# A routing search that starts tighter: next expert's first span from the running expert's first round, three rounds instead of four for experts 3 to 5

## The chip, the cores and the metric

One NeuronCore of one Trainium2 chip. The metric is the device time of one execution in microseconds (us); the kernel before takes 852.79 us, the median of three runs (852.39 to 853.32). Engine names: PE is TensorE (PEld its weight loads), DVE is VectorE, ACT is ScalarE, POOL is GpSimd, SP is SyncE.

## The reference

Windowed attention with sink tokens gives `x` (3072 tokens of 512). A first mixture of experts (top one of eight by `x @ w_gate + bias`) replaces `x`. A second mixture, the one that matters here, gives every one of its eight experts exactly `cap` = 384 tokens, greedily by score:

```python
logits = x @ w_gate
order = np.argsort(-logits.flatten())
for idx in order:
    tok, e = idx // E, idx % E
    if assigned[tok] >= 0 or counts[e] >= cap: continue
    assigned[tok] = e; counts[e] += 1
for e in range(E):
    mask = assigned == e
    out[mask] = np.maximum(x[mask] @ w1[e], 0) @ w2[e]
```

## The kernel before

**Order of the work.** Attention, then the first mixture, then the second (`moe2`, from about 497 us on). In `moe2` the eight experts' feed-forward blocks run one after the other in the order in which the experts fill up; expert k below means the k-th to fill. Each block has eight steps (`Ffn.run`); a step is 12 matmuls of the first layer (L1036) and 9 of the second (L950), all in three-way split fp32. During the last two steps of a block the rows of the next expert are transposed on PE (L796) after three indirect gathers on POOL have fetched them (L1893).

**The routing.** It is not done ahead: `Route.steps` is a generator that is advanced between groups of matmuls of the blocks, so that expert k+1 and k+2 are searched while expert k computes. For each expert it searches the score at which the best-filled expert reaches 384 tokens. One round of the search divides the present span into 62 parts: DVE forms `ub` and compares it with 64 marks (`compare`, L1678 and L1679, the tile `cmp`), PE counts with 13 matmuls (`count`, L1693), DVE compares the counts with 384 (`gs`, `gg`), PE sums over partitions with one matmul (L1976), DVE takes the maxima (`J8`, one value per expert in falling order) and forms the new lower end `lo`. Between rounds POOL copies one number (`hold`, L1957): it depends on DVE's `b0`, so POOL, which works in order, does not begin what is queued behind it (the weight splits L901 and L922) until DVE has done its comparison. Then the expert's rows are marked (`A`), turned into a list of indices by `compact_steps` (L1498, L1517, L1523, `idx`), and POOL gathers them.

**Number of rounds.** `NIT` is 4. Expert 0 takes three rounds (1 to 3, the first was done earlier by `Route.pre`), experts 1 and 2 take three (0 to 2), experts 3 to 6 take four (0 to 3), expert 7 gets what is left. The lower end of expert k's first span is `lb[k]`, from the one coarse round of `Route.pre`; its upper end is the threshold of expert k-1.

**What sets the order.** Every instruction is queued by hand-written order. A planner (`Clock`, `Vec`) counts the matmul columns as PE time and adds for each routing instruction on DVE 0.12 us and 1.04 ns for each element of its free size. After each piece of the routing the generator yields the planned time at which its next piece may be queued (`yield clk.dve + CM[...]`, `CM` 0.2, 1.3, 1.3). `Route.pop`, called several times in each step, queues the next piece if that time has come and DVE is not planned ahead of PE by more than `SLACK`. Gathers for expert j are queued when its list is ready and the blocks have come to step 8j-9 (`poll_x`, `XO`).

The instructions of `steps`, `compact_steps` and others that are recorded through `Vec` all carry L145 in the profile (the helper's line), so that they are told apart by their tiles.

Of the kernel before, what the change touches and what calls it, by code (L numbers as in the profile page):

```python
# [15 lines left out]
OP = mybir.AluOpType  # L16
# [9 lines left out]
E, F = 8, 1024  # L26
# [32 lines left out]
def bc(ap, shape):  # L59
    return ap.to_broadcast(shape)  # L60


class K:
    def __init__(self):
        self.clk = Clock()
# [1401 lines left out]
JC, NIT, FEW, IDLE = 64, 4, 2, (3, 2, 1)  # L1467
WARM, WARM1, WA = 9, 3, (7, 4, 3, 2)
SLACK = 0.5
SLACK1 = 1.6  # L1470
XO = 9
X0 = 2.0
# [78 lines left out]
class Route(Src):  # L1551
# [4 lines left out]
    def __init__(self, nc, g, pool, xs):  # L1556
        self.nc, self.g, self.p, self.xs = nc, g, pool, xs
        self.e, self.regs, self.idx, self.x = {}, {}, {}, {}
        self.gen = self.steps()
        self.comp = []  # L1560
        self.em3 = {}
        self.at = [0.0, 0.0]
        p = pool
        self.L = p.tile([128, NR, E], F32, name="L")
        self.LG = p.tile([128, NSUB, E], F32, name="LG")
        self.ent = p.tile([128, NSUB, 2], I32, name="ent")
        self.pn = p.tile([128, NMAIN], F32, name="pn")
        self.vb = p.tile([128, NMAIN], BF, name="vb")
        self.tki = p.tile([128, 3, NMAIN], I32, name="tki")
        self.S_ = p.tile([128, NR], F32, name="S_")  # L1570
        self.OH = p.tile([128, NR, E], BF, name="OH")
        self.ub = p.tile([128, NR], BF, name="ub")
        self.cmp = p.tile([128, 2, JC, HR], BF, name="cmp")
        self.cuts = ((0, HA), (HA, HT + 1))
        self.cmp2 = [p.tile([128, 2, JC, e - o], BF, name=f"cmp{o}") for o, e in self.cuts]
        self.T = p.tile([128, NR], F32, name="T_")
        self.sc = p.tile([128, 20], F32, name="sc")
        self.fl = p.tile([128, E], F32, name="fl")
        self.lb = p.tile([128, E], F32, name="lb")
        self.pad = p.tile([128, SSML], F32, name="pad")  # L1580
        self.pw = p.tile([128, NIT], F32, name="pw")
        self.dd1 = p.tile([128, 4, NIT], F32, name="dd1")
        self.hold = p.tile([1, NIT], F32, name="hold")
        self.of = p.tile([2, 128], F32, name="of")
        self.z = p.tile([128, 128], BF, name="z")
        self.r = p.tile([128, 4, NR], F32, name="r0")
        self.gg = p.tile([128, E], BF, name="gg")
        self.gg2 = p.tile([128, 2, E], BF, name="gg2")
        self.tm = p.tile([128, NR], F32, name="tm")
        self.chk = p.tile([128, 3, E], F32, name="chk")  # L1590
        self.want = p.tile([128, 3, E], F32, name="chw")
        (self.lo0, self.lo, self.lop, self.b0, self.b1, self.J, self.esum, self.eidx, self.bad, self.t0, self.nbig, self.span,
         self.half, self.nrow, self.hi, self.J2, self.nv) = (self.sc[:, i:i + 1] for i in range(17))

    def setup(self):

# [56 lines left out]
    def sizes(self, V, pd):  # L1653
        V.tensor_reduce(self.half, pd, axis=AX.X, op=OP.max)
        V.tensor_scalar(self.nbig, self.half, 1e-20, -16.0, op0=OP.max, op1=OP.mult)
        V.tensor_scalar(self.half, self.nbig, 0.5, None, op0=OP.mult)
        V.tensor_scalar(self.nrow, self.nbig, 2.0, None, op0=OP.mult)

    def widths(self, V, dd, o, span):
        V.tensor_scalar(dd[:, 0, o:NIT], self.pw[:, 0:NIT - o], span, 1e-30, op0=OP.mult, op1=OP.max)  # L1660
        V.reciprocal(dd[:, 1, o:NIT], dd[:, 0, o:NIT])
# [167 lines left out]
    def pop(self):  # L1829
        clk = self.g.clk  # L1830
        for i, f in ((1, self.pop_comp), (0, self.pop_main)):
            if clk.pe >= self.at[i] and clk.dve < clk.pe + (SLACK if 1 in self.idx else SLACK1):
                f()
# [80 lines left out]
    def steps(self):  # L1914
        nc, g, p = self.nc, self.g, self.p
        clk = g.clk
        V = Vec(nc, clk)
        ioE = g.iota[:, 0:E]
        L, S_, OH, cmp, chk, tm = self.L, self.S_, self.OH, self.cmp, self.chk, self.tm
        lo, lop, b0, b1, esum, eidx, bad, t0, nbig, span, half, nrow = (  # L1920
            self.lo, self.lop, self.b0, self.b1, self.esum, self.eidx, self.bad, self.t0, self.nbig, self.span,
            self.half, self.nrow)
# [5 lines left out]
        J8 = p.tile([128, E], F32, name="J8m")  # L1928
        J = J8[:, 0:1]
        dn = None  # L1930
        for k in range(E):
# [4 lines left out]
            if k < E - 1:  # L1936
                dd = self.dd1 if k == 0 else dn
                lo0 = self.lb[:, k:k + 1]
                first = 1 if k == 0 else 0
                last = NIT - 1 if k == 0 or k > FEW else NIT - 2  # L1940
                for it in range(first, last + 1):
                    d, inv = dd[:, 0, it:it + 1], dd[:, 1, it:it + 1]
                    if k == 0:
                        if it > first:
                            V.scalar_tensor_tensor(self.ub, bc(dd[:, 2, it - 1:it], [128, NR]), J, self.T, op0=OP.mult, op1=OP.add)
                            self.against(V)
                            V.scalar_tensor_tensor(lo, J, dd[:, 0, it - 1:it], b0, op0=OP.mult, op1=OP.add)
                        if it < last:
                            V.tensor_scalar(b1, dd[:, 3, it:it + 1], lo, None, op0=OP.add)
                            V.tensor_scalar(self.T, S_, b1, dd[:, 1, it + 1:it + 2], op0=OP.subtract, op1=OP.mult)  # L1950
                        if it == first:
                            V.tensor_scalar(b0, d, -1.5, lo, op0=OP.mult, op1=OP.add)
                    else:
                        self.compare(V, slice(0, 2), slice(0, HR), inv)
                        V.tensor_scalar(b0, d, -1.5, lo0 if it == 0 else lo, op0=OP.mult, op1=OP.add)
                        if it > 0:
                            nc.gpsimd.tensor_copy(self.hold[:, it - 1:it], b0[0:1])  # L1957
                        if it < last:
                            V.tensor_scalar(b1, dd[:, 0, it + 1:it + 2], -128.0, b0, op0=OP.mult, op1=OP.add)
                    if k == 0 and it == first + 1:  # L1960
                        z = self.z
                    self.fill((0 if k == 0 else WT[7] if k == 1 else WT[0]) if it == first else WT[9 if it == first + 2 else 0] if k == 0 else WT[8])
                    yield clk.dve + CM[min(k, 2)]
                    self.count(pn, range(HT + 1), k == 0 and it > first)
                    clk.mm(64 * (HT + 1))
                    if it == first:
                        nc.tensor.matmul(pc, g.ones, OH, start=True, stop=True, skip_group_check=True)
                        nc.scalar.activation(junk, pc, AF.Copy, accum_out=chk[:, 0, k:k + 1])
                    gg = self.gg
                    V.tensor_scalar(gs, pn[JC:2 * JC, E:2 * E], -1.0, float(CAP) - 0.5, op0=OP.mult, op1=OP.add)  # L1970
                    V.tensor_tensor(gg[0:JC], pn[0:JC, 0:E], gs, op=OP.is_ge)
                    if k == 0 and it > first:
                        V.tensor_scalar(b0, d, -1.5, lo, op0=OP.mult, op1=OP.add)
                    self.fill(WT[1])
                    yield clk.dve + 0.2
                    nc.tensor.matmul(pb, g.ones, gg, start=True, stop=True, skip_group_check=True)  # L1976
                    V.max(J8, pb)
                    if k == 0 and it == first + 1:
                        nc.tensor.matmul(self.cbank[:, 0:64], z, z[:, 0:64], start=True, stop=True, skip_group_check=True)
                    if k > 0:  # L1980
                        if it < last:
                            V.scalar_tensor_tensor(lop, J, d, b1, op0=OP.mult, op1=OP.add)
                        V.scalar_tensor_tensor(lo, J, d, b0, op0=OP.mult, op1=OP.add)
# [297 lines left out]
```

## Time and profile before

| | us |
|---|---|
| median of three runs | 852.79 |
| profiled execution, its time | 853.57 |
| profiled execution, its span | 851.8 |
| PE busy | 813.5 (96%) |
| DVE busy | 608.7 (71%) |
| POOL busy | 348.0 (41%) |

The span is what the trace covers; 1.8 us of the profiled execution lie outside it. A window of the trace gives the busy time of each engine in a stretch, a timeline gives the instructions of an engine in order, with the idle time just before an instruction and what ended it in brackets.

### The profile page before, as it was taken

Reading aid. Unit: us, or ns where it says so; the run is one execution under the profiler, and the core shown is the slowest. Engines: PE = TensorE matmul, PEld = TensorE weight load, DVE = VectorE, ACT = ScalarE, POOL = GpSimd, SP = SyncE. Lnnn points to the kernel's source line nnn. Section 1 sums busy time; section 2 is a strip of 40 time slices with the busy share of each in tenths; the row PEclk is TensorE's granted clock in tenths of the full one; section 3 lists DMA queues with packets and bytes.
Section 4 is the critical chain, followed back from the end, with each engine's and each line's share of the span. In section 5 each row is a group of like instructions: output and inputs, shape, how many; then the busy total and the mean of one; then the engine's idle time right before and its main releaser. Section 6 shows DMA issues by size and latency. Waiting matters only on the chain.

```text
span 851.8 us, 15197 instructions
## 1 busy us (share of the span) xinstructions
PE 813.5 (96%) x5001; PEld 651.6 (76%) x5006; DVE 608.7 (71%) x1763; ACT 384.9 (45%) x1091; POOL 348.0 (41%) x574
## 2 busy tenths in 40 slices
PE   8889999998999999999999988999999999999997
PEld 4666666667888888888888746778888888889996
DVE  7888787877579696978878268868688787753320
ACT  6667777764342433344342313334334343434442
POOL 5455967582331101020000004436465656465662
PEclk9999999999999999999999998999999999999999
DMA  7434555666534544444436507334444345345401
GB/s 222 159 107 150 151 144 143 176 217 215 120 84 166 161 136 149 149 148 126 124 104 223 192 14 235 126 110 149 145 155 146 129 151 154 126 161 174 147 39 42
DMA packets 70655, 122.85 MB, mean 144 GB/s; under 512 B 9890, under 2 KB 24102, under 8 KB 70440
## 3 DMA queue, kind: packets, MB, share of 16 engines
q1 hardware_dynamic: 63848, 102.36, 38.0%
q0 software_dynamic: 6720, 19.43, 7.1%
q8 instruction: 42, 0.69, 0.4%
q14 instruction: 45, 0.37, 0.2%
HBM read 102.06 MB, written 19.71 MB: 143 GB/s over the span
## 4 chain that ended last, share of the span: by engine, by line
PE 78%; DVE 11%; ACT 4%; issue 3%; DMA 1%; POOL 1%; DVEq 0%; POOLq 0%; ACTq 0%
PE y L950 29%; PE ph L1036 28%; PE sp L323 4%; PE po L395 3%; ACT P L352 3%; PE tr L796 2%; PE rt L1693 2%; PE pt L360 2%; PE px L431 1%; PE rc L1523 1%; DMA xg<-xs,idx 1%; DVE mx L342 1%; DVE sc L145 1%; PE sp L409 1%; DVE sp L340 1%
## 5 line engine op out<-in xcount | busy, mean ns | idle before, releaser
L1046 ACT ACTIVATE hh<-ph 128x384 fp32r<-128x384 f32 (+1 forms) x112 | 60.2, 538 | 268.2 <-PE ph L1036 267.6
L1036 PE MATMUL ph<-xh,w1h 128*128 128x384 f32 (+1 forms) x448 | 166.9, 372 | 0.8 <-DVE hl L1047 0.8
L1036 PE MATMUL ph<-xh,w1l 128*128 128x384 f32 (+1 forms) x448 | 161.1, 360 | 1.2 <-DVE w1l L922 1.2
L1036 PE MATMUL ph<-xl,w1h 128*128 128x384 f32 (+1 forms) x448 | 160.4, 360 | 0.0
L950 PE MATMUL y<-w2h,hh 128*128 128x512 f32 x384 | 153.6, 400 | 0.0
L950 PE MATMUL y<-w2h,hl 128*128 128x512 f32 x384 | 150.9, 393 | 0.0
L950 PE MATMUL y<-w2l,hh 128*128 128x512 f32 x384 | 150.5, 392 | 0.0
L1047 DVE SCALAR_TENSOR_TENSOR hl<-ph,hh 128x384 fp32r<-128x384 f32 (+1 forms) x112 | 68.4, 612 | 98.6 <-ACT hh L1046 98.1
L1201 POOL DMA_INDIRECT xg<-xd,ent x26 | 28.0, 1078 | 195.0 <-DMA ent<-idtab 189.8
L1225 DVE SCALAR_TENSOR_TENSOR junk<-yr,wgb 128x512 f32<-128x512 f32 x160 | 103.1, 685 | 0.0
L901 POOL TENSOR_TENSOR w2l<-w2r,w2h 128x512 fp32r<-128x512 f32 x60 | 79.2, 1326 | 46.1 <-ACT w2h L897 22.2
L1036 PEld LDWEIGHTS ph<-xh,w1h 128*128 128x128 f32 x448 | 85.0, 190 | 12.6 <-issue 1.9
L1036 PEld LDWEIGHTS ph<-xh,w1l 128*128 128x128 f32 x448 | 84.3, 188 | 11.1 <-DVE w1l L922 1.6
L352 ACT ACTIVATE P<-sp,mx 128x132 f32<-128x132 f32 x192 | 69.3, 369 | 51.5 <-DVE mx L342 18.7
L1036 PEld LDWEIGHTS ph<-xl,w1h 128*128 128x128 f32 x448 | 84.0, 188 | 7.7
L950 PEld LDWEIGHTS y<-w2h,hl 128*128 128x128 f32 x384 | 72.0, 188 | 15.6
L950 PEld LDWEIGHTS y<-w2h,hh 128*128 128x128 f32 x384 | 72.6, 189 | 11.5 <-issue 0.2
L950 PEld LDWEIGHTS y<-w2l,hh 128*128 128x128 f32 x384 | 72.2, 188 | 11.7
L323 PE MATMUL sp<-kr,qs 64*128 64x260 f32 (+1 forms) x384 | 58.6, 402 | 13.7 <-ACT P L352 12.5
L917 ACT ACTIVATE w1h<-w1r 128x512 fp32r<-128x512 f32 x108 | 67.3, 624 | 2.1 <-DVE lp L449 2.1
L897 ACT ACTIVATE w2h<-w2r 128x512 fp32r<-128x512 f32 x108 | 67.5, 625 | 0.0
L922 DVE TENSOR_TENSOR w1l<-w1r,w1h 128x512 fp32r<-128x512 f32 x78 | 63.8, 818 | 2.4 <-ACT w1h L917 2.4
(394 smaller groups left out, 1401.9 us busy)
## 6 DMA issues: line engine op xcount, KB each, us to landing
w1r<-in_w_dram SPq DMA_DIRECT2D x29, 1024.0 KB, 5.8
w2r<-in_w_dram SPq DMA_DIRECT2D x29, 1024.0 KB, 5.9
vr<-in_v_dram SPq DMA_DIRECT2D x16, 384.0 KB, 4.9
xd<-xb SPq DMA_DIRECT2D x16, 384.0 KB, 3.5
xs<-yr SPq DMA_DIRECT2D x24, 256.0 KB, 6.1
kr<-in_kT_dram SPq DMA_DIRECT2D x15, 396.0 KB, 3.8
qr<-in_qT_dram SPq DMA_DIRECT2D x15, 384.0 KB, 4.3
wgb<-in_wg2T_dram SPq DMA_DIRECT2D x1, 2048.0 KB, 8.4
```

The costliest lines, as they stand in the source:

```text
L323: nc.tensor.matmul(sp[:, hd, c0:260], qs[o:o + 64, 128 * i:128 * i + 128], kr[o:o + 64, k0:k0 + 260 - c0], start=True, stop=True)
L352: nc.scalar.activation(z.P[:, n % 2, hd, :], s.sp[:, hd, 128:260], AF.Exp, bias=s.mx[:, hd:hd + 1], accum_out=z.sm[:, n % 2, hd:hd + 1])
L897: nc.scalar.activation(ch[1][c][0], r[q // 2][:, q % 2, :] if isinstance(r, list) else r[:, q, :], AF.Copy)
L901: eng.tensor_tensor(lo, r[q // 2][:, q % 2, :] if isinstance(r, list) else r[:, q, :], h.bitcast(F32), op=OP.subtract)
L917: nc.scalar.activation(h, v, AF.Copy)
L922: eng.tensor_tensor(lo, v, h.bitcast(F32), op=OP.subtract)
L950: nc.tensor.matmul(o, l, r, start=(first and i == 0), stop=(end and i == 2))
L1036: nc.tensor.matmul(ph, wp[:, c, :], xp_[:, c, 0:NTK], start=(d == 0 and i == 0), stop=(d == 3 and i == len(cut[d]) - 1))
L1046: nc.scalar.activation(hh, ph, AF.Relu)
L1047: nc.vector.scalar_tensor_tensor(hl, ph, 0.0, hh.bitcast(F32), op0=OP.max, op1=OP.subtract)
L1201: self.nc.gpsimd.indirect_dma_start(out=self.xg[j][:, a, :], out_offset=None, in_=self.G.xd[0:k, :], in_offset=bass.IndirectOffsetOnAxis(a ...
L1225: nc.vector.scalar_tensor_tensor(junk, yr[:, 0:DM], 1.0, wgb[:, e, :], op0=OP.mult, op1=OP.mult, accum_out=lg[:, e:e + 1])
```

## The change

One more instruction in `sizes` (once, before the routing begins) sets `least`, 0.04 of the largest score. In round 1 of experts 1 to 4 four more DVE instructions, each on a column of 128 numbers, raise the lower end `lb` of the next expert: the second-best expert's lower end after round 0, or the running expert's present lower end less `least`, whichever is lower, and never below the old one (if no second expert has reached 384 anywhere, the old one stays). Experts 3, 4 and 5 take three rounds instead of four. Expert 6 keeps four, experts 0, 1 and 2 keep three.

```diff
+LEAST = 0.04
@@ __init__
-         self.half, self.nrow, self.hi, self.J2, self.nv) = (self.sc[:, i:i + 1] for i in range(17))
+         self.half, self.nrow, self.hi, self.J2, self.nv, self.next, self.least, self.none) = (self.sc[:, i:i + 1] for i in range(20))
@@ sizes
+        V.tensor_scalar(self.least, self.nbig, -LEAST / 16.0, None, op0=OP.mult)
@@ steps
-                last = NIT - 1 if k == 0 or k > FEW else NIT - 2
+                last = NIT - 1 if k in (0, E - 2) else NIT - 2
...
                         self.compare(V, slice(0, 2), slice(0, HR), inv)
+                        if it == first + 1 and k < E - 3:
+                            low = self.lb[:, k + 1:k + 2]
+                            V.tensor_scalar(self.none, J8[:, 1:2], 0.5, nbig, op0=OP.is_lt, op1=OP.mult)
+                            V.tensor_scalar(self.next, J8[:, 1:2], dd[:, 0, first:it], b0, op0=OP.mult, op1=OP.add)
+                            V.scalar_tensor_tensor(self.next, lo, self.least, self.next, op0=OP.subtract, op1=OP.min)
+                            V.scalar_tensor_tensor(low, self.next, self.none, low, op0=OP.add, op1=OP.max)
                         V.tensor_scalar(b0, d, -1.5, lo0 if it == 0 else lo, op0=OP.mult, op1=OP.add)
```

## Rows read from the trace of the kernel before

**Rows 1.** The page's first part: engine, busy us (share of span), instructions.

```profile
PE 813.5 (96%) x5001; PEld 651.6 (76%) x5006; DVE 608.7 (71%) x1763; ACT 384.9 (45%) x1091; POOL 348.0 (41%) x574
```

**Rows 2.** Windows of 20 us: length, busy us of each engine, PE clock, DMA.

```profile
core 0: us, PE busy (x) PEld busy (x) DVE busy (x) ACT busy (x) POOL busy (x), PEclk, DMA share, GB/s
600.00:620.00 20.00, 20.00 (x115) 17.59 (x116) 15.66 (x47) 9.92 (x22) 8.83 (x11) 1.00 0.45 157
...
660.00:680.00 20.00, 18.93 (x143) 16.36 (x142) 15.61 (x38) 5.80 (x15) 13.37 (x14) 1.00 0.40 137
...
780.00:800.00 20.00, 20.00 (x103) 18.14 (x102) 5.29 (x8) 9.03 (x18) 12.42 (x12) 1.00 0.50 186
```

**Rows 3.** Timeline of PE, one round of expert 4: start, us, instruction.

```profile
629.36 0.95 PE L1693 MATMUL rt<-OH,cmp 128*128 128x16 bf16 x13
630.16 0.42 PE L1036 MATMUL ph<-xh,w1h 128*128 128x384 f32 x1
630.42 0.34 PE L1036 MATMUL ph<-xh,w1l 128*128 128x384 f32 x1
630.60 0.33 PE L1036 MATMUL ph<-xl,w1h 128*128 128x384 f32 x1
...
631.29 0.18 PE L1976 MATMUL rt<-gg,ones 128*128 128x8 bf16 x1
631.34 0.43 PE L1036 MATMUL ph<-xh,w1h 128*128 128x384 f32 x1
631.60 0.34 PE L1036 MATMUL ph<-xh,w1l 128*128 128x384 f32 x1
```

**Rows 4.** Timeline of PE, the fourth rounds' counts of experts 3, 4 and 5.

```profile
607.90 0.95 PE L1693 MATMUL rt<-OH,cmp 128*128 128x16 bf16 x13
...
643.93 0.96 PE L1693 MATMUL rt<-OH,cmp 128*128 128x16 bf16 x13
...
682.42 0.95 PE L1693 MATMUL rt<-OH,cmp 128*128 128x16 bf16 x13
```

**Rows 5.** Timeline of PE and its weight loads: instructions that waited, idle in brackets.

```profile
529.74 0.45 PE L1036 MATMUL ph<-xh,w1h 128*128 128x384 f32 x1 [0.79 <-DVE hl L1047]
...
555.25 0.33 PE L796 MATMUL tr<-cst,xg 128*128 128x128 f32 x1 [1.13 <-DMA xg<-xs,idx]
...
563.34 0.31 PEld L796 LDWEIGHTS tr<-cst,xg 128*128 128x128 f32 x3 [0.55 <-DVE xl L798]
...
599.96 0.33 PE L796 MATMUL tr<-cst,xg 128*128 128x128 f32 x1 [1.02 <-DMA xg<-xs,idx]
...
676.68 0.95 PE L1693 MATMUL rt<-OH,cmp 128*128 128x16 bf16 x13 [1.07 <-DVE cmp L145]
...
735.90 0.26 PE L2033 MATMUL rc<-OH,ones 128*128 128x224 bf16 x1 [0.68 <-DVE OH L145]
```

**Rows 6.** Timeline of DVE: routing instructions on one column.

```profile
576.66 0.21 DVE L145 TENSOR_TENSOR sc<-sc,lb 128x1 f32<-128x1 f32 x1
576.90 0.23 DVE L145 TENSOR_SCALAR dd<-pw,sc 128x4 f32<-128x4 f32 x1
...
593.40 0.35 DVE L145 SCALAR_TENSOR_TENSOR sc<-J8m,dd,sc 128x1 f32<-128x1 f32 x2
...
672.11 3.18 DVE L145 SCALAR_TENSOR_TENSOR sc<-J8m,dd,sc 128x1 f32<-128x1 f32 x2
```

**Rows 7.** Timeline of DVE behind round 1 or 2's comparison, experts 1, 2, 3.

```profile
529.14 1.01 DVE L1047 SCALAR_TENSOR_TENSOR hl<-ph,hh 128x384 fp32r<-128x384 f32 x2
...
562.74 0.55 DVE L798 TENSOR_TENSOR xl<-tr,xh 128x384 fp32r<-128x384 f32 x1
...
590.75 0.76 DVE L145 SCALAR_TENSOR_TENSOR idx<-pj 128x3 int32<-128x3 f32 x2
```

**Rows 8.** Timeline of POOL: a hold, a gather for expert 2, a weight split.

```profile
589.99 0.18 POOL L1957 COPY hold<-sc 1x1 f32<-1x1 f32 x1 [1.54 <-DVE sc L145]
...
592.82 1.02 POOL L1893 DMA_INDIRECT xg<-xs,idx  x1 [0.16 <-issue]
...
673.86 1.28 POOL L901 TENSOR_TENSOR w2l<-w2r,w2h 128x512 fp32r<-128x512 f32 x1
```

## The prediction

> **What bounds the kernel now.** I read the page's first part, then windows of 20 us over the second mixture, then the timelines of PE, DVE and POOL there. PE is busy 96% of the span [rows 1]. [...] So what the change takes out of PE's queue counts nearly one for one, unless PE then waits instead. The few waits are read one by one, since each is a place where a later DVE or POOL instruction moves the end. Between the start of the routing and its end those that matter are [rows 5]: 0.79 us for `hl` in expert 0's first steps; 1.13 for the last of expert 1's gathered rows (and a little less for those before them); 0.55 at a weight load, about half of it idle on PE, for `xl` at 563.34; 1.02 for expert 2's gathered rows; 1.07 for a `cmp` of expert 5; 0.68 for expert 7's `OH`. After the last list there is none: the window from 780 to 800 us is full and has no routing in it [rows 2].
>
> **What is removed.** Three rounds: the fourth ones of experts 3, 4 and 5, with their counts at 607.90, 643.93 and 682.42 [rows 4]. What a round costs PE is read from [rows 3]. The 13 counts push the block from 629.36 to 630.16, 0.80 us; the block's next two matmuls then start 0.26 apart instead of 0.18, so 0.08 more; the sum over partitions takes 0.05 (631.29 to 631.34) and again leaves a pitch of 0.26, 0.08 more. That is 1.01 us a round, 3.0 us for three. The lower bound leaves the late starts out, 0.85 a round or 2.6; the upper one takes the two full busy times, 0.95 + 0.18 = 1.13 or 3.4. The DVE work of these rounds (a comparison and some eight short instructions) and three POOL holds of 0.18 us [rows 8] go too. I cost those at nothing: DVE and POOL have idle time beside a full PE (15.66 and 8.83 busy of 20 us [rows 2]), and the places where DVE holds PE up are priced below.
>
> Each removed round also ends its expert's search earlier, by about 7 us (629.36, expert 4's round 1, to 643.93, its round 3, are 14.6 us for two [rows 3, 4]). That brings nothing by itself: PE waits for the gathered rows of experts 1 and 2 alone [rows 5], whose searches keep their three rounds, and the later gathers aren't queued before step 8j-9 in any case.
>
> **What is added.** Four DVE instructions on one column in round 1 of experts 1 to 4, between the comparison and `b0`. A dependent instruction of this size starts 0.24 us after the one it needs (576.66 to 576.90); two independent ones take 0.35 together, so with 0.22 for one of them they start about 0.13 apart [rows 6]. The first two are independent of each other, the third needs the second, the fourth the third, and `b0` needs none: 0.13 + 0.24 + 0.24 + 0.13 = 0.7 us a round. Bounds: 4 x 0.13 = 0.5 and 4 x 0.24 = 1.0. The comparison comes before them, so PE's count doesn't wait; what waits is what stands behind them on DVE, and on POOL behind the hold, which needs `b0`:
> - Expert 1: `hl` at 529.14 carries no idle time of DVE ahead of it [rows 7], so it starts when the routing's instructions before it are done, and it ends PE's stall of 0.79 [rows 5]. I take the whole 0.7.
> - Expert 2: `xl` at 562.74, without idle ahead of it either [rows 7], is the next but three behind round 1's comparison, and PE's transposes wait for it at 563.34 [rows 5]. The wait exists already, so again 0.7.
> - Expert 3: expert 2's list `idx` is finished at 590.75 to 591.5, behind round 1's comparison [rows 7]; the hold at 589.99 follows `b0`, two splits follow the hold, the gather at 592.82 follows these [rows 8]. All move by 0.7, and with them the stall of 1.02 [rows 5]: 0.7.
> - Expert 4: no stall hangs on its round 1: 0, up to 0.7.
>
> Sum 2.1 us; bounds 0 (if the reordering below puts other work there) and 2.8 (four places). The instruction in `sizes` is one more of at most 0.24, in the first mixture's tail, ahead of a comparison that PE awaits: 0.1, bounds 0 and 0.24.
>
> [...]
>
> **What is moved.** The planner counts 4 x 0.12 = 0.48 us more of DVE in each of these rounds, so the next piece may be queued later. The places for a piece lie three matmuls apart, 0.53 us at the pitch of 0.18 [rows 3] and a little more in the second layer, so most such pieces go one place later, three times before the gather of expert 2. Where the search is on the path to a gather, that adds up to 0.6 each time; where a piece moves behind an `hl` it takes the stall for that `hl` away. Bounds -0.8 and +1.8. I take +0.5, nearer to zero, since two of the three places are paid by the DVE delay already.
>
> **The stalls that may go.** The 1.07 at 676.68 comes from one collision: two `sc` instructions that take 0.35 us elsewhere took 3.18 at 672.11 [rows 6], until POOL's split ended at 673.86 + 1.28 = 675.14 [rows 8]. With two rounds fewer by then, POOL's splits and this round no longer meet in the same way. The 0.68 at 735.90 is a wait for DVE too. New meetings are as possible as the old ones were, and there were two. I count -0.9, half of the two together; bounds -1.75 and +1.0.
>
> **The sum.** -3.0 + 2.1 + 0.1 + 0.5 - 0.9 = -1.2 us. The profiled execution (853.57, of it 851.8 span) would come to 852.4; it lies 0.8 above the median of the runs, and the same 1.2 off that median, 852.79, gives 851.6.
>
> **The rivals.**
> - *PE's whole saving comes through.* The later pieces fall into places where DVE has slack, one of the three 0.7 us is paid, and both late stalls go: -3.0 + 0.7 - 1.75 = -4.0, 848.8. For it: PE is full, and three rounds are certainly gone. Against: at three places PE waits already for what is delayed. 0.25.
> - *The added instructions eat it all.* All three places are paid, each piece goes one place later, and the late stalls only change their places: -3.0 + 2.1 + 0.1 + 1.8 = +1.0, 853.8. For it: the search of experts 1 and 2, which loses no round, is the part that PE waits for. Against: it needs the bound of each term on one side. 0.13.
> - *Slower, by POOL's splits.* The holds come 0.7 us later, and so do the splits behind them; an `sc` of the round that follows, ahead of expert 2's gather, then falls under two splits and takes 3.18 - 0.35 = 2.8 us longer, as at 672.11 [rows 6, 8]. Without the gain on the late stalls the sum stands at -0.3, and one such place makes +2.5, 855.3; it decides from about 2 us on. Against: while the new instructions run POOL stands idle at the hold, 1.54 us of it at 589.99 [rows 8], and a split that starts later also leaves more of the round behind it. 0.12. [...]
> - *It doesn't do what it says.* If three rounds from the tighter span could not isolate 384 tokens, the flag `bad` would send the kernel through the general path, far slower than any number here. I worked the search out from the reference's inputs: the first spans of experts 3 to 5 come to about 0.04 of the largest score (0.04 to 0.89 before), the third round's step to 1.7e-7 of it, and each count to 384. Under 0.01.
>
> **How the numbers follow.** Forecast 0.50 (its own spread about -2.6 to 0 us), rivals 0.25, 0.13, 0.12. The range goes from the first rival's time to most of the way to the slower one's: 848.8 to 854.8. The chances are for a difference of over 0.2%, 1.7 us, about what a measurement of this kernel can tell from none: faster is the first rival and a third of the forecast's spread, 0.41; slower the third rival and a little of the second, 0.13; the rest 0.46.
>
> **What would show it.** 22 sums over partitions instead of 25, no fourth count for experts 3 to 5, 13 holds instead of 16, about 3 us less busy time on PE. The wait for expert 2's rows 0.7 to 1.9 us longer, the wait for `hl` in expert 0 changed by 0.7 either way, that for `xl` at expert 1's transposes longer. The wait of 1.07 for `cmp` gone or elsewhere. Expert 6's list a good 15 us earlier, and the blocks after it unchanged. I am wrong if the waits ahead of 600 us don't grow, or if a new one of over 1 us stands among the later rounds.

## The result and the profile after

The changed kernel takes 866.02 us (median of five runs, 865.05 to 866.95); the kernel before, run beside it, 853.32 (852.39 to 853.91). The ratio is 1.014, with a 95% interval of 1.0121 to 1.0159: 12.7 us slower, where 1.2 us faster was forecast and the range ended at 854.8. The profiled execution took 866.2, with a span of 864.5.

The page's first part of the kernel after:

```profile
PE 816.8 (94%) x4959; PEld 655.3 (76%) x4964; DVE 603.8 (70%) x1753; ACT 385.5 (45%) x1091; POOL 345.4 (40%) x571
```

and windows of 20 us of it (length, busy us of each engine, clock granted to PE, DMA):

```profile
660.00:680.00 20.00, 17.61 (x125) 15.11 (x124) 13.96 (x31) 7.60 (x17) 14.95 (x19) 1.00 0.43 141
680.00:700.00 20.00, 14.80 (x79) 12.66 (x78) 15.35 (x38) 5.27 (x13) 3.61 (x3) 0.83 0.18 61
700.00:720.00 20.00, 20.00 (x139) 17.24 (x137) 10.79 (x32) 7.00 (x14) 11.26 (x15) 0.91 0.50 156
720.00:740.00 20.00, 18.10 (x103) 15.36 (x102) 15.03 (x42) 7.15 (x20) 11.09 (x10) 0.91 0.40 135
```

and windows of the kernel before, for the stretch that [rows 2] leave out:

```profile
680.00:700.00 20.00, 20.00 (x116) 17.41 (x116) 16.60 (x39) 8.92 (x21) 9.78 (x9) 1.00 0.37 116
700.00:720.00 20.00, 20.00 (x148) 17.35 (x147) 15.48 (x41) 7.79 (x18) 13.11 (x16) 1.00 0.54 175
720.00:740.00 20.00, 19.32 (x113) 16.91 (x112) 16.56 (x44) 8.84 (x21) 9.41 (x9) 1.00 0.33 106
```

PE is busier in all (816.8 against 813.5 [rows 1]) although three rounds are gone, and its share is smaller. Both come from one stretch: between 680 and 700 us it stands still for 5.2 us, and for 60 us its matmuls have a mean granted clock of 0.83 to 0.91 where the kernel before has 1.00. `xl` and `hl` are the low parts that DVE forms of the transposed rows and of the first layer's output; PE needs both. Which wait it is, the timeline of PE shows (start, us, instruction, in brackets the idle time before it and what ended it):

```profile
530.96 0.44 PE L1036 MATMUL ph<-xh,w1h 128*128 128x384 f32 x1 [0.95 <-DVE hl L1047]
...
565.43 0.55 PE L796 MATMUL tr<-cst,xg 128*128 128x128 f32 x3 [0.93 <-DVE xl L798]
...
644.55 0.55 PE L796 MATMUL tr<-cst,xg 128*128 128x128 f32 x3 [1.20 <-DVE xl L798]
...
678.47 0.16 PE L1499 MATMUL rc<-rs,tri 128*128 128x1 bf16 x1 [2.38 <-DVE A L145]
...
692.66 0.90 PE L796 MATMUL tr<-cst,xg 128*128 128x128 f32 x3 [5.20 <-DVE xl L798]
...
694.21 0.63 PE L950 MATMUL y<-w2h,hl 128*128 128x512 f32 x1
...
725.32 0.26 PE L2041 MATMUL rc<-OH,ones 128*128 128x224 bf16 x1 [1.90 <-DVE OH L145]
```

The first two answer to the 0.79 for `hl` and the 0.55 for `xl` in [rows 5], and the last is the 0.68 for expert 7's `OH`, grown to 1.90. The three between them, 1.20, 2.38 and 5.20, are new. The second x transposes of expert 4, at 692.66, wait for `xl` of the first ones, since both use one PSUM tile, `tr`. Why `xl` is late stands in DVE's timeline of the kernel after:

```profile
672.01 6.40 DVE L145 SCALAR_TENSOR_TENSOR A<-S__77,sc,oe 128x28 bf16<-128x28 f32 x1
...
679.31 1.51 DVE L145 SCALAR_TENSOR_TENSOR L<-ce,sc,L 128x224 f32<-128x224 bf16 x1
...
684.07 2.11 DVE L145 TENSOR_TENSOR cmp<-ub,iou 128x1792 bf16<-128x1792 bf16 x1
...
687.49 1.09 DVE L145 TENSOR_TENSOR ohb<-iob,rb 128x1792 bf16<-128x1792 bf16 x1
688.50 1.57 DVE L145 TENSOR_TENSOR ft<-r,tcr 128x336 bf16<-128x336 f32 x1
...
690.46 1.08 DVE L145 TENSOR_TENSOR ohb<-iob,rb 128x1792 bf16<-128x1792 bf16 x1
691.46 0.68 DVE L922 TENSOR_TENSOR w1l<-w1r,w1h 128x512 fp32r<-128x512 f32 x1
692.06 0.55 DVE L798 TENSOR_TENSOR xl<-tr,xh 128x384 fp32r<-128x384 f32 x1
```

From 672.01 to 692.06 DVE has no idle time at all. Ahead of `xl` stand the marking of expert 5's tokens (`A`), the update of the scores (`L`, `OH`), expert 6's first comparison (`cmp`) and the whole compaction of expert 5 (`ohb`, `ft`); this piece is called the burst below. `A` takes 6.40 us. POOL's timeline of the same time:

```profile
672.00 0.17 POOL L1965 COPY hold<-sc 1x1 f32<-1x1 f32 x1
672.14 1.29 POOL L901 TENSOR_TENSOR w2l<-w2r,w2h 128x512 fp32r<-128x512 f32 x1
673.39 1.28 POOL L922 TENSOR_TENSOR w1l<-w1r,w1h 128x512 fp32r<-128x512 f32 x1
674.64 2.50 POOL L901 TENSOR_TENSOR w2l<-w2r,w2h 128x512 fp32r<-128x512 f32 x2
677.11 1.25 POOL L922 TENSOR_TENSOR w1l<-w1r,w1h 128x512 fp32r<-128x512 f32 x1
```

Five splits end at 678.36, and `A` ends when they do. In the kernel before `xl` of the same rows comes ahead of all this:

```profile
684.88 0.56 DVE L798 TENSOR_TENSOR xl<-tr,xh 128x384 fp32r<-128x384 f32 x1 [1.11 <-ACT xh L797]
...
686.96 0.56 DVE L798 TENSOR_TENSOR xl<-tr,xh 128x384 fp32r<-128x384 f32 x1 [0.47 <-ACT xh L797]
...
689.62 0.25 DVE L145 SCALAR_TENSOR_TENSOR A<-S__77,sc,oe 128x28 bf16<-128x28 f32 x1
```

Where the loss arises is read from the first x transposes of each expert. Expert 3's come at 641.10 (640.81 before), expert 4's at 685.22 (683.83), expert 5's at 740.92 (724.62). Expert 5's in PE's timeline of the kernel after:

```profile
740.92 0.49 PE L796 MATMUL tr<-cst,xg 128*128 128x128 f32 x3
```

and of the kernel before:

```profile
724.62 0.49 PE L796 MATMUL tr<-cst,xg 128*128 128x128 f32 x3
```

So 16.0 us are lost between 641 and 741 us, beside 0.3 ahead of it; 3.6 come back later, 3.05 of them in expert 5's block (36.64 us to the next first transposes, before 39.69), because the last lists are done earlier, and 12.7 are left. Idle time of PE is the larger part: in the windows from 640 to 740 us it is busy 89.2 us, before 98.25, so it stands idle for 9.05 more. The lower clock is the other part. Windows of the kernel after show a granted clock of 0.50 from 692.70 to 698.50 and from 705.30 to 708.50, and 0.54 from 725.50 to 728.70. At full clock these stretches would have been shorter by 2.9, 1.6 and 1.5 us, an estimate from the granted clock, 6.0 together. The 1.0 that is left fits the routing work that now stands ahead of 741 us, about the 3.05 that come back, less two removed rounds of 1.01.

### The profile page after: what moved, and what is told of

Same layout as the page of the kernel before. It is cut to its first block, busy times and chain, and to the rows that moved or that the text cites. A ratio compares the mean times of both kernels' runs of the same rounds, so it can differ in the third digit from the quotient of the medians.

```text
span 864.5 us, 15108 instructions
## 1 busy us (share of the span) xinstructions
PE 816.8 (94%) x4959; PEld 655.3 (76%) x4964; DVE 603.8 (70%) x1753; ACT 385.5 (45%) x1091; POOL 345.4 (40%) x571
## 4 chain that ended last, share of the span: by engine, by line
PE 74%; DVE 16%; ACT 4%; issue 4%; POOL 1%; DMA 0%; DVEq 0%; POOLq 0%; ACTq 0%
PE y L950 27%; PE ph L1036 27%; PE sp L323 4%; ACT P L352 3%; PE po L395 3%; PE tr L796 2%; PE rt L1695 2%; PE pt L360 2%; PE px L431 1%; PE rc L1524 1%; DVE sc L145 1%; DVE mx L342 1%; DVE cmp L145 1%; PE sp L409 1%; DVE A L145 1%
```

## The experiments

Three theories stood at first. A: without the fourth round's hold POOL runs its splits in one row, and the row falls on `A`. B: the four added instructions are the cause. C: the shorter search reaches marking and compaction at another place of the block, ahead of `xl`. Later expectations call A' the wider form of A, the supposition that the splits stretch any two-input instruction of DVE that they fall on.

**Three rounds alone.** The kernel before, with

```diff
-                last = NIT - 1 if k == 0 or k > FEW else NIT - 2
+                last = NIT - 1 if k in (0, E - 2) else NIT - 2
```

> The kernel before with three rounds for experts 3 to 5 and nothing else: no instruction is added, the spans are not tightened, each third round still ends on 384 tokens for these inputs. Theory A (the fewer holds and the earlier rounds put an unbroken row of POOL weight splits on top of expert 5's marking instruction A, which locks DVE out for several us): the POOL queue is that of the changed kernel, so A of expert 5 takes 4 us or more again and the time is 861 to 866, below the changed kernel by no more than the 2 to 3 us of the added instructions. Theory B (the added DVE instructions and their reordering of the early rounds cause the loss): 849 to 851.5, no A over 1.3 us.

864.19 us, ratio 1.012 (1.009 to 1.0151). Its timelines of DVE and PE:

```profile
674.57 6.37 DVE L145 SCALAR_TENSOR_TENSOR A<-S__77,sc,oe 128x28 bf16<-128x28 f32 x1
...
695.14 0.90 PE L796 MATMUL tr<-cst,xg 128*128 128x128 f32 x3 [3.76 <-DVE xl L798]
```

Nearly the whole loss is there without an added instruction: B falls.

**The added instructions alone.** The kernel after, with the old line for `last` in place of the new one.

> The changed kernel with four rounds for experts 3 to 6 as before, so the added instructions alone. Theory A: POOL keeps its holds in the rows of the kernel before, no A over 1.3 us, and the time is 853.5 to 856 (the price of four instructions in each of four rounds). Theory B: 862 or more.

855.55 us against 853.19 for the kernel before on that chip: 2.4 us, ratio 1.0023 (1.0003 to 1.0044, which is 0.3 to 3.8 us). PE's waits for `hl` and `xl` in experts 0 and 1 are 0.94 and 0.93, and one for `xl` of expert 2's rows is 0.95. No `A` is long.

**A hold behind the marking.** The kernel after, with

```diff
                 V.tensor_scalar(em, eidx[0:1], float(E - 1), None, op0=OP.min)
+                if 2 < k < E - 2:
+                    nc.gpsimd.tensor_copy(self.hold[:, NIT - 2:NIT - 1], eidx[0:1])
```

> The changed kernel with one more POOL hold for experts 3, 4 and 5, queued where the marking is done and waiting for the expert's number, so that at most the splits queued before it can meet A. Theory A: in the row of splits behind expert 4's gathers two stand before the new hold, so A of expert 5 falls from 6.4 us to 1.3 to 2.8 us, PE's wait for xl of 5.2 us goes to under 2, the clock stays at its upper level there, and the time is 854 to 860. Theory C (it is not the row of splits; the routing simply comes at a bad point of the block, with the gathers and transposes): within 2 us of the changed kernel, 864 to 868.

864.77 us, ratio 1.0134 (1.0093 to 1.0175). `A` is short, and the wait for it is gone, but not the loss; timelines of DVE and PE:

```profile
673.04 2.31 DVE L145 SCALAR_TENSOR_TENSOR sc<-J8m,dd,sc 128x1 f32<-128x1 f32 x1
...
676.25 0.25 DVE L145 SCALAR_TENSOR_TENSOR A<-S__77,sc,oe 128x28 bf16<-128x28 f32 x1
...
678.49 1.27 DVE L145 SCALAR_TENSOR_TENSOR tm<-A,sc,tm 128x28 f32<-128x28 bf16 x1
...
681.12 1.36 DVE L145 TENSOR_TENSOR OH<-L,S__77 128x224 bf16<-128x224 f32 x1
...
688.54 1.56 DVE L145 TENSOR_TENSOR ft<-r,tcr 128x336 bf16<-128x336 f32 x1
...
692.69 0.90 PE L796 MATMUL tr<-cst,xg 128*128 128x128 f32 x3 [4.83 <-DVE xl L798]
```

The splits fall on other instructions of the same burst instead, and `xl` is as late as it was. Theory A in this form (the row on `A`) falls.

**Four rounds for expert 5 again.** The kernel after, with

```diff
-                last = NIT - 1 if k in (0, E - 2) else NIT - 2
+                last = NIT - 1 if k in (0, E - 3, E - 2) else NIT - 2
```

> The changed kernel with four rounds kept for expert 5 as well as for expert 6, so only two rounds are removed and a hold stands again two splits behind expert 4's gathers. Theory A: A of expert 5 moves to behind the fourth round, takes 0.25 us there, the collision costs no more than the 3 us of the kernel before: 852 to 856. Theory B: 862 or more. Theory C: 858 or more, since round 1 of expert 5 still lies before the stores and the gathers.

864.77 us, ratio 1.0139 (1.0111 to 1.0168). `A` takes 0.25 here, PE waits 2.83 us for `xl` at 691.08 and 2.36 for `gg` at 725.91. A round put back at one expert moves the collision; it doesn't remove it.

**The same rounds, at another place.** The kernel after, with a request to be called again later, for which no engine waits:

```diff
+                if k in (3, 4, 5):
+                    yield clk.pe + 6.5
                 ce = p.tile([128, E], BF, name="ce")
```

> The changed kernel, with one thing added: for experts 3, 4 and 5 the routing gives back control and asks to come again 6.5 us of the planner's TensorE time later, after the third round's last sum and before the marking of the expert's tokens. No engine waits for it; it only puts the rest of the routing behind other work in the queues. In the instruction order this puts the token split of the next x rows (xl) ahead of the compaction of expert 5 again, as in the kernel before; in the changed kernel xl stood behind marking, both compare steps and all of the compaction. Theory C (the loss is the place in the block at which the shorter routing arrives, so that compaction and the next expert's first comparison stand ahead of xl on VectorE): the waits for xl of 5.2 us and the low clock behind them go, and the time is 851 to 854 us: three rounds saved (-3.0 us) and the four added instructions three times (+2.4 us by the run with them alone). Theory A' (the loss comes from GpSimd's weight splits, which without the fourth round's hold run in unbroken rows over the two-input instructions of VectorE): the holds stay removed, so the rows of splits stay, and the time stays above 860 us.

851.13 us against 853.45, ratio 0.9973 (0.9958 to 0.9989). In 640 to 740 us PE waits for one thing, 0.67 us for `OH`. Timelines of DVE:

```profile
684.16 0.56 DVE L798 TENSOR_TENSOR xl<-tr,xh 128x384 fp32r<-128x384 f32 x1 [2.20 <-ACT xh L797]
...
686.25 0.56 DVE L798 TENSOR_TENSOR xl<-tr,xh 128x384 fp32r<-128x384 f32 x1 [0.47 <-ACT xh L797]
...
687.70 0.73 DVE L145 SCALAR_TENSOR_TENSOR A<-S__77,sc,oe 128x28 bf16<-128x28 f32 x1
```

Neither the rounds nor the holds are back, and the loss is gone: the 15 us go with the place, as C says. POOL's rows of splits are three long here, not five, so this run alone doesn't clear POOL.

**Three rounds alone, at another place.** The kernel of the first run, with the same request, 7 us.

> Three rounds instead of four for experts 3 to 5, without the added instructions, and with the same request to come again later (7 us here, which gives the same order of xl and compaction). It has the three rounds removed and nothing else that costs an engine time. Theory C: three rounds of 1.0 us less on TensorE than the kernel before, 850 to 852 us, a ratio of 0.996 to 0.999, where three rounds alone gave 864. Theory A' (unbroken rows of GpSimd splits): the splits of the removed rounds are still without a hold, 860 us or more. A third way: the saving of a removed round is nothing, because TensorE waits for the weights' splits or x anyway: 853 us, the time of the kernel before.

849.89 us (849.0 to 853.37) against 853.45, ratio 0.9948 (0.9929 to 0.9967). It beats both kernels: 3.6 us for three rounds by the medians, 2.8 to 6.1 by the interval, where the same kernel without the request lost 11.0.

**No reading splits on POOL.** In the second mixture, for the kernel after and for the kernel before:

```diff
-                eng.tensor_tensor(lo, v, h.bitcast(F32), op=OP.subtract)
+                if eng is nc.gpsimd:
+                    for _ in range(2):
+                        eng.memset(lo.bitcast(F32), 0.0)
+                else:
+                    eng.tensor_tensor(lo, v, h.bitcast(F32), op=OP.subtract)
```

and the same for the second layer's splits.

> The changed kernel with every weight split of GpSimd in the second mixture layer (a subtraction that reads two operands in SBUF) replaced by two memsets of the same tile; the low parts of those weights are left out. GpSimd keeps its place in the orders and reads nothing. If GpSimd's reads lock out VectorE's two-input instructions and this is the root of the loss (A'), the marking instruction falls from 6.4 us to 0.25, the waits for xl fall below 1.5 us, and the time comes within 3 us of the kernel before with the same replacement. If the order alone is the root (C without A'), the burst of VectorE work ahead of xl shrinks only by the few stretched instructions (6.1 us marking, about 1 us each at L and the comparison), xl still waits about 2 us or more, and the distance to the kernel before with the same replacement stays at 5 us or more.

> The kernel before with the same replacement, as the base for the run of the changed kernel with it. The stretched VectorE instructions of the kernel before (3.18 us for two of 0.2, 2.21 for a comparison of 1.09) go. Both theories: 849 to 853 us, as nearly none of them stood on TensorE's path; below 848 us would show that GpSimd's reads cost time in the kernel before as well.

848.53 us after, 848.58 before. The change costs nothing here, though its order of work is that of the kernel after, all of the burst ahead of `xl`. Timeline of DVE, kernel after without reading splits:

```profile
669.54 0.25 DVE L145 SCALAR_TENSOR_TENSOR A<-S__77,sc,oe 128x28 bf16<-128x28 f32 x1
...
674.70 1.09 DVE L145 TENSOR_TENSOR cmp<-ub,iou 128x1792 bf16<-128x1792 bf16 x1
...
680.19 0.68 DVE L930 TENSOR_TENSOR w1l<-w1r,w1h 128x512 fp32r<-128x512 f32 x1
681.31 0.56 DVE L798 TENSOR_TENSOR xl<-tr,xh 128x384 fp32r<-128x384 f32 x1 [0.44 <-ACT xh L797]
```

From `A` to the end of `w1l` the burst takes 680.87 - 669.54 = 11.3 us, where the kernel after takes 692.14 - 672.01 = 20.1, and `xl` waits for ACT, no longer for the burst. The stretched instructions make the difference: `A` 6.40 against 0.25, `L` 1.51 against 0.43, `cmp` 2.11 against 1.09, `ft` 1.57 against 0.50, together 9.3 us. So, by this pair and the two runs at another place, it takes both: the burst ahead of `xl`, and POOL's splits that stretch it. The memsets are somewhat shorter than the splits (1.10 us a pair against 1.28), so POOL runs a little less in this pair than it does otherwise.

**A late search with four rounds.** The kernel before, with

```diff
+                if k in (4,):
+                    yield clk.pe + 18.0
                 ce = p.tile([128, E], BF, name="ce")
```

> The kernel before, all four rounds kept and no added instruction; after expert 4's last round the routing asks to come again 18 us of the planner's TensorE time later. In the order of VectorE's instructions this puts marking, comparison and the whole compaction of expert 5 ahead of the first x split of the expert whose rows are transposed next, as the changed kernel has it at 670 to 692 us. Theory C with the splits (a burst of VectorE work ahead of xl, stretched by GpSimd's splits, is what costs; the number of rounds only decides where it falls): waits for xl of 2 us or more, a stretch of lower granted clock, 858 to 866 us. If removing rounds is itself the cause (fewer holds, GpSimd's rows): 853 to 855 us, the time of the kernel before.

876.08 us, ratio 1.0264 (1.0236 to 1.0293), but for another reason than the one to be tested; timeline of PE:

```profile
686.05 0.45 PE L796 MATMUL tr<-cst,xg 128*128 128x128 f32 x1 [4.30 <-DMA xg<-xs,idx]
```

18 us later, the list of the rows themselves is too late (first gather at 682.50), and PE waits for the gather, not for `xl`. The run says nothing on the burst; it shows that such a delay has a limit.

**Work for PE in the wait.** The kernel after, with 50 matmuls that nobody reads ahead of the transposes at 692.66:

```diff
+        self.busy = None
...
+        if (j, d) == (4, 1) and self.busy is not None:
+            b = self.busy()
+            for _ in range(50):
+                nc.tensor.matmul(b, self.g.wz[:, 0:128], self.g.wz[:, 0:224], start=True, stop=True, skip_group_check=True)
...
+        f.busy = lambda: rt.cbank[:, 256:480]
```

> The changed kernel with 50 matmuls of 224 columns on a spare part of a PSUM bank ahead of the second x transposes of the fifth expert in the row, where TensorE stood still for 5.2 us; at full clock they take about 50 x 0.093 = 4.7 us, so they fill that wait and make TensorE no later. Nobody reads them. If the lower granted clock behind the wait (0.66 of full in 690 to 700 us) comes from the idle time and costs what its matmuls show (692.7 to 698.5 us took 5.8 us, about 3.3 at full clock; perhaps 705.3 to 708.5 too, 3.2 against 1.8), the clock in 690 to 700 is near 1.00 and the time 2 to 4 us below the changed kernel's 866: 862 to 864 us. If the low clock has another cause, it stays, and the time is 866 us or above.

862.52 us, ratio 1.0104 (1.0075 to 1.0133), 3.5 us less than the kernel after; it is 8.5 above the kernel before beside it (854.04), where the kernel after was 12.7 above. PE's timeline:

```profile
688.60 4.96 PE L798 MATMUL rc<-wz 128*128 128x224 bf16 x50
693.40 0.49 PE L801 MATMUL tr<-cst,xg 128*128 128x128 f32 x3
...
694.19 0.40 PE L955 MATMUL y<-w2h,hl 128*128 128x512 f32 x1
...
697.23 0.49 PE L801 MATMUL tr<-cst,xg 128*128 128x128 f32 x3
```

and its windows:

```profile
680.00:700.00 20.00, 18.71 (x137) 16.81 (x137) 16.95 (x46) 6.28 (x15) 6.60 (x6) 1.00 0.24 78
700.00:720.00 20.00, 20.00 (x147) 17.36 (x146) 11.77 (x41) 7.71 (x17) 12.18 (x16) 1.00 0.54 185
720.00:740.00 20.00, 19.12 (x118) 16.62 (x117) 16.71 (x38) 7.96 (x19) 11.47 (x9) 1.00 0.33 106
```

The 50 matmuls take 4.80 us from the start of the first to that of the next transposes, 0.096 each, where 0.093 was expected. The granted clock is 1.00 in all three windows, where the kernel after has 0.83, 0.91 and 0.91 (in 660 to 680 us it is 0.91 here and 1.00 there). From the second to the third x transposes it is 3.83 us here (693.40 to 697.23) and 6.18 in the kernel after (692.66 to 698.84): 2.35 us are the price of the low clock at this one place. Its profiled execution has the wait of 2.38 for `A` no longer, so not all of the 3.5 us need be the clock's: the splits fall on an `sc` ahead of `A` there, which takes 3.52 us, and `xl` still comes at 692.35.

**The request for expert 3 alone.** The kernel after, with the request of 6.5 us at `k == 3` only.

> As the run with the request to come again 6.5 us later, but after expert 3's third round only. In the order, expert 5's marking then still stands ahead of the x splits in question, but its compaction (two comparisons of 1.1 us, ft) behind the first three of them. If it is the whole burst that costs, marking alone ahead of xl costs little: 851 to 855 us. If marking (with its 6.4 us under GpSimd's splits) ahead of xl is enough: 858 us or more.

857.63 us, ratio 1.0039 (1.0023 to 1.0056): between the two expectations, and nearer to the worse. With `xl` ahead of the compaction the wait for it is 1.20 at 685.87, but the marking and the lists that come later collide in their turn; PE's and DVE's timelines:

```profile
712.59 3.36 DVE L145 TENSOR_SCALAR ub<-S__77,sc,dd 128x28 bf16<-128x28 f32 x1
...
725.91 0.26 PE L2043 MATMUL rc<-OH,ones 128*128 128x224 bf16 x1 [2.84 <-DVE OH L145]
```

The place has to be right for each expert, not for one.

## Why the prediction was wrong

- *A removed round is worth 1.01 us on PE.* Held: three rounds in good places brought 3.6 us (849.89 against 853.45; 2.8 to 6.1 by the interval), against the 3.0 of the sum and its upper bound of 3.4. Sums fell from 25 to 22 and holds from 16 to 13, as said.
- *The four added instructions cost 0.7 us at three places, 2.1 in all*, 2.7 with `sizes` and what is moved. The sum fits: alone they cost 2.4, 0.3 to 3.8 by the interval. In the kernel after the first of them starts at 523.30 and the `sc` behind them at 524.12, 0.82 us. That is near the 0.7 that the pitches of [rows 6] gave. The places fit less well, so that the sum came out near is partly luck. Only the wait for `xl` at 565.43 came as named (0.93, where the two runs with three rounds alone have 0.38 at most). The wait for `hl` is 0.95, but these two runs, without an added instruction, have 0.96 and 0.94. The one for expert 2's rows didn't grow: 0.72 for `xl` of the same rows stands in its place.
- *A shorter search "brings nothing by itself".* This is the step that failed. It was asked only whether the gathers come earlier, and expert 4's don't (668.35 instead of 667.72). That marking, update, comparison and compaction also come earlier (`A` of expert 5 at 672.01 instead of 689.62, 17.6 us), and that this puts them ahead of `xl` in DVE's queue instead of behind it, was not asked. With it fell "I cost those at nothing": the idle time of DVE was read as an average of windows (15.66 of 20 us [rows 2]), while what counted was one piece of routing ahead of an instruction that PE awaits: 11.3 us of it without the splits' reads cost nothing there, 20.1 us under them held PE up for 5.20.
- *The stalls that may go: -0.9, at worst +1.0.* The 1.07 for `cmp` did go; new meetings came, and one of them was 6.4 us on a marking of 0.25. The bound was drawn from how long one meeting with splits had been in the trace of before (3.18 us [rows 6]), and a row of five splits is not bounded by that. With the splits' reads gone the change costs nothing (848.53 against 848.58), near the -0.3 that the sum gives without this term.
- *Slower, by POOL's splits.* What this rival feared, DVE instructions that take longer while POOL splits, is what came, at another place and through another door: not an `sc` ahead of expert 2's gather that a later hold exposes, but `A`, `L`, `cmp` and `ft` of the burst ahead of `xl`, with 9.3 us instead of 2.8. It had 0.12 and a price of 2.5 us over before; 12.7 came.
- *The clock* stood in no term. All prices were read at the 1.00 of [rows 2], but there PE had hardly waited (20.00, 18.93 and 20.00 of 20 us busy). After a wait of 5.20 us the clock was 0.50 until 698.50 and again from 705.30 to 708.50, 2.35 us at the one place that was measured directly and about 6.0 in all by the estimate above.
- The "new one of over 1 us among the later rounds", which was to show the prediction wrong, is what came: 1.20, 2.38 and 5.20 us, and 1.90 where 0.68 had been. Busy time on PE, which was to fall by about 3 us, rose by 3.3.

Still open: whether the place alone, with four rounds, would cost as much, since the run meant for that waited for gathers; and why the clock fell from 705.30 to 708.50, where PE had not waited since 692.66. In the run with work for PE in the wait it was 1.00 there.

## What to carry to other kernels

Removing work from a hand-ordered queue moves all that follows it: before a gain is booked, list what now stands ahead of each instruction that the bottleneck engine awaits, and add up its length with the neighbours' interference in it. A burst that hides behind a full engine at one place can be exposed 18 us earlier; here one line that asks to be called 6.5 or 7 us later turned a loss of 11 to 13 us into a gain of 2 to 4. An average of idle time in a window doesn't show whether a burst fits.

## What the runs showed of the hardware

- A DVE instruction of 0.25 us took 6.40 while POOL ran five subtractions with SBUF operands without a gap, and ended with the last of them (678.41 and 678.36). With memsets in their place `A` took 0.25, and no routing instruction of DVE was over 1.1 us. Not only instructions with two inputs were stretched: in the kernel before `ub`, with one input beside its columns, began at 654.89 under a split and took 0.84, until that split ended (655.73 and 655.70), where its usual time is 0.29.
- The same splits cost the kernel before too: 848.58 us without their reads, against 853.45 (ratio 0.9935, 0.9915 to 0.9955), though the longest wait of PE for DVE in [rows 5] is 1.07. Without the reads none of its PE's waits behind 527 us is over 0.33. The memsets are shorter than the splits, too, so how much of this is the reads' alone is not shown.
- After 5.2 us of standing still the granted clock was 0.50, and PE's matmuls of 512 columns started 0.43 us apart instead of 0.23, from 692.70 to 698.50; with useless matmuls in the wait the clock was 1.00 and they kept 0.23. That wait was thus dearer than its length. A drop is not always due to a wait: in 660 to 680 us the kernel after with the request has 0.91 with PE busy for the whole 20.00 us.
